# A new written order for the first two chunks of a fused attention and feed-forward kernel, with nine normalizing multiplications on GpSimd

## The chip, the cores and the metric

The kernel runs on one core of one Trainium2 chip. A core has five engines that matter here: TensorE (PE, matrix products), VectorE (DVE), ScalarE (ACT), GpSimd (POOL) and SyncE (SP), whose queue issues all loads and stores of this kernel. Every engine works through its own queue strictly in order; an instruction that waits holds up everything queued behind it on that engine, and nothing on the others. The metric is the device time of one execution in microseconds (us), lower is better.

## The reference

The reference computes attention for 4 batches, 8 heads, 768 rows and head size 64, and then a feed-forward layer on the 3072 rows of 512 that come out.

```python
k_sum = k.reshape(B, H, nb, 32, D).max(axis=3)          # 24 block maxima of the keys
v_sum = v.reshape(B, H, nb, 32, D).mean(axis=3)         # 24 block means of the values
scores_l = scale * q @ k.T, masked to |i - j| < 16      # window
scores_s = scale * q @ k_sum.T + log(32)
a = exp(concat(scores_l, scores_s) - rowmax)
a = a / (sum(a) + 1e-9)
x = a @ concat(v, v_sum)
h = x @ w_in;  r = max(h, 0);  g = s * r * r + b;  out = g @ w_out    # 512 -> 2048 -> 512
```

Inputs and output are float32. The products of the feed-forward layer are made to nearly full precision: each factor is split into an upper part and a remainder (in the tile type fp32r), and three products are summed, upper by upper, upper by remainder and remainder by upper.

## The kernel before

**Tiling.** The 3072 rows are cut into 12 chunks of 256 (three to a batch). A chunk passes through two stages. The attention stage goes by four pairs of heads `p`: for each, scores on PE, mask and row minimum on DVE, `exp` with row sums on ACT, normalization, a turn of the weights (by PE transposes in the first three chunks), and the products with the values on PE. A window of 96 keys and the 24 block maxima make rows of 120 weights; a pair's normalized tile `pr` is 128 x 4 x 120, that is 128 x 480. The feed-forward stage goes by 16 slices `f` of the inner dimension (128 wide): 12 products of 256 columns for the hidden rows, then for each two slices relu, square, scale and split, then 6 products of 512 columns for each slice into the output sums.

**Weights.** The weights come as raw 64-bit integers in the memory's layout, slice by slice (512 KB for each of the two sides). For each slice ACT rescales the two halves of the words (lines 122, 123), DVE joins them to a float (131, 132), DVE or ACT makes the upper part `wh` (219, 221 in a shared copy helper) and DVE the remainder `wl` (144). The hidden product of slice `f` cannot start before `wl` of that slice is there. This happens once, while the first two chunks run; later chunks find the weights in SBUF.

**What sets the order.** There is no scheduler: instructions are issued in the order in which the Python code calls the functions, and so each engine's queue is a piece of that order. For chunk 2's feed-forward stage and all later chunks the order comes from a table of steps. For chunks 0 and 1, together with the attention of chunk 2 and the first scores of chunk 3, it is written out by hand as a string of 450 names, `FIRST_ORDER`. A letter names the function, numbers its arguments (chunk, pair or slice), and asterisks choose another engine for the operation:

- `q` loads keys and queries of chunk 0, `u` those of later chunks, `x`, `v` the value windows, `r` whole value rows, `i`, `o`, `w` the weights of a slice (in, out, both), `s` copies the two scalars on POOL.
- `K` block maxima (DVE), `k` their copies into a pair's key tile (POOL), `Z`, `S` scores (PE), `M` mask (DVE, L323), `E` exps (ACT, L336), `N` normalize, `T` transposes (PE, L379), `C` copies the turned weights out (ACT, or DVE with an asterisk), `V`, `U` products with values and means (PE), `R`, `F` block means of the values (PE, then ACT or DVE), `t` their copies into a value window (POOL, L263), `X`, `y` upper part and remainder of the attention's result (`xh`, `xl`; L433 is `y` on DVE).
- `A`, `B`, `D`, `h`, `l` are the steps of the weights: rescale on ACT, join on DVE (halves and whole), upper part (ACT, or DVE with an asterisk), remainder on DVE.
- `Y`, `H` hidden products (PE; `Y` those of slices 0 and 1 of chunk 0 by pieces), `J` relu and square, `G` scale, `a`, `b` split, `P` output products (PE, L516), `O` copies the sums out and stores them, `W` a few products that only keep PE running.

`N` has three instructions: an addition of 1e-9 on 128 x 4 sums (L343), a reciprocal on DVE (L344) and the multiplication of the 128 x 480 tile (L346). In the kernel before an asterisk puts the addition on POOL, and the reciprocal and the multiplication are always on DVE.

**Places that the prediction speaks of.** `y1.3` is the last remainder of chunk 1's attention result, the eighth L433 row on DVE; it releases the hidden products of chunk 1 (`H1.0`, the first L460 row on PE). `V1.3` is chunk 1's last product with values; it waits for `t1.3`, a POOL copy. From `H1.0` on, PE has only large products in its queue with a little attention of chunks 2 and 3 between.

Of the kernel before, what the change touches and what calls it, by code (L numbers as in the profile page):

```python
# [19 lines left out]
P = 128  # L20
# [24 lines left out]
def windowed_attention_then_relu2_ffn(ctx, tc, qk, vwin, kt, vt, kq, vrow, wp, out):  # L45
# [107 lines left out]
    def k_max(bi, p):  # L153
        ksum[bi, p] = p2.tile([P, NB], F32, name="ksum", bufs=12)
        raw = kraw[bi, p]
        nc.vector.tensor_reduce(
            ksum[bi, p], raw.rearrange("p (n t) -> p n t", t=BLOCK), axis=AX.X, op=ALU.max
        )
# [181 lines left out]
    def normalize(c, p, other=False):  # L340
        mn_of.pop((c, p))
        rs = p2.tile([P, 4], F32, name="rs")
        (nc.gpsimd if other else nc.vector).tensor_scalar(rs, sm_of.pop((c, p)), 1e-9, None, ALU.add)  # L343
        nc.vector.reciprocal(rs, rs)  # L344
        pr = pr_of[c, p]
        nc.vector.tensor_tensor(pr, pr, rs.unsqueeze(2).to_broadcast([P, 4, KR]), ALU.mult)  # L346
# [186 lines left out]
    def evict(c, t, other=False):  # L533
# [184 lines left out]
```

## Time and profile before

| | us |
|---|---|
| median of 3 runs | 610.28 (610.14 to 610.51) |
| profiled execution | 611.14 |
| its span, from the first to the last instruction | 609.40 |
| PE busy in the span | 598.2 (98%) |
| DVE busy | 418.6 (69%) |
| ACT busy | 275.7 (45%) |
| POOL busy | 139.6 (23%) |

The granted TensorE clock is 1.00 in every stretch. A row of the timeline has the start, the duration, engine, source line, operation, the tile written and the tile read, the shape, how many instructions the row merges, and in square brackets how long the engine had been idle and what released it. A row of the groups has busy time and mean duration in ns behind the bar, then the idle time in front. A start of a following instruction can lie up to 0.1 us before the end of the one in front, since ends overlap.

### The profile page before, as it was taken

What the parts mean: (1) busy time and instruction counts of PE and PEld (TensorE: products, weight loads), DVE (VectorE), ACT (ScalarE), POOL (GpSimd) and SP (SyncE); (2) the same over time, 40 slices, a digit from 0 to 9 for tenths busy, and PEclk for the clock granted to TensorE, in tenths of its full rate; (3) what the DMA queues carried; (4) which work ended last, traced back from release to release, by engine and by line L of the source; (5) the groups of instructions that cost most, each with busy time, mean ns of one, the idle gap of its engine ahead of it and who ended that gap; (6) DMA issues with size and microseconds to landing.
All of it is one profiled execution on the core that took longest, in us unless ns stands there. A gap on an engine that the chain in (4) does not pass through costs nothing.

```text
span 609.4 us, 13484 instructions
## 1 busy us (share of the span) xinstructions
PE 598.2 (98%) x5240; PEld 539.5 (89%) x5240; DVE 418.6 (69%) x1126; ACT 275.7 (45%) x712; POOL 139.6 (23%) x275
## 2 busy tenths in 40 slices
PE   7999999999999999999999999999999999999997
PEld 6798988989888998999889899998998998898896
DVE  6999898789579368758858657847858827832211
ACT  5999898262362263163144244325235236223221
POOL 4420012211421411411041321231141151141110
PEclk9999999999999999999999999999999999999999
DMA  8998723026305015203502211600710500200000
GB/s 340 395 401 358 277 77 113 1 71 166 127 3 185 1 45 198 85 20 104 170 21 80 107 45 40 243 18 2 227 67 2 187 2 19 87 1 1 36 2 35
DMA packets 26993, 66.41 MB, mean 109 GB/s; under 512 B 3824, under 2 KB 3824, under 8 KB 26928
## 3 DMA queue, kind: packets, MB, share of 16 engines
q1 hardware_dynamic: 26928, 65.54, 30.3%
q8 instruction: 41, 0.67, 0.4%
q14 instruction: 24, 0.20, 0.1%
HBM read 59.09 MB, written 6.29 MB: 107 GB/s over the span
## 4 chain that ended last, share of the span: by engine, by line
PE 84%; ACT 7%; DVE 4%; issue 2%; DMA 2%; POOL 1%; SPq 0%; POOLq 0%; DVEq 0%; ACTq 0%
PE po L516 40%; PE ph L460 37%; PE pav L417 4%; PE ps L301 3%; ACT wraw L122 1%; ACT pr L336 1%; ACT wraw L123 1%; DVE wl L144 1%; DMA vsum<-vmean 1%; DVE wf L132 1%; POOL vw L263 1%; DMA kq<-in_kq_dram 1%; ACT r L468 1%; DVE wf L131 0%; PE pt L379 0%
## 5 line engine op out<-in xcount | busy, mean ns | idle before, releaser
L481 POOL TENSOR_SCALAR r<-r,sb_col 128x512 f32<-128x512 f32 x85 | 69.9, 823 | 386.5 <-ACT r L474 249.6
L468 ACT ACTIVATE r<-ph 128x512 f32<-128x512 f32 x93 | 55.5, 597 | 199.4 <-PE ph L460 144.0
L516 PE MATMUL po<-wh,gl 128*128 128x512 f32 x384 | 132.2, 394 | 0.0
L368 DVE STREAM_TRANSPOSE pT<-pr 32x256 f32<-32x256 f32 x288 | 125.4, 436 | 4.2
L460 PE MATMUL ph<-xh,wl 128*128 128x256 f32 x760 | 118.8, 279 | 0.5 <-ACT r L468 0.3
L460 PE MATMUL ph<-xl,wh 128*128 128x256 f32 x760 | 117.6, 277 | 0.0
L460 PE MATMUL ph<-xh,wh 128*128 128x256 f32 x760 | 117.4, 277 | 0.0
L460 PEld LDWEIGHTS ph<-xh,wl 128*128 128x128 f32 x760 | 104.7, 188 | 5.8 <-ACT r L474 0.7
L460 PEld LDWEIGHTS ph<-xl,wh 128*128 128x128 f32 x760 | 101.1, 188 | 0.0
L460 PEld LDWEIGHTS ph<-xh,wh 128*128 128x128 f32 x760 | 100.6, 188 | 0.0
L516 PEld LDWEIGHTS po<-wh,gl 128*128 128x128 f32 x384 | 72.1, 188 | 14.9 <-issue 1.1
L219 DVE CAST gha<-r 128x512 fp32r<-128x512 f32 x45 | 19.6, 437 | 89.1 <-POOL r L481 88.9
L336 ACT ACTIVATE pr<-pr,mn 128x120 f32<-128x120 f32 x176 | 67.0, 382 | 22.8 <-DVE mn L323 22.7
L516 PE MATMUL po<-wh,gha 128*128 128x512 f32 x192 | 75.3, 392 | 0.0
L516 PE MATMUL po<-wl,gha 128*128 128x512 f32 x192 | 75.3, 392 | 0.0
L516 PE MATMUL po<-wl,ghb 128*128 128x512 f32 x192 | 75.0, 391 | 0.0
L516 PE MATMUL po<-wh,ghb 128*128 128x512 f32 x192 | 75.0, 390 | 0.0
L474 ACT ACTIVATE r<-r 128x512 f32<-128x512 f32 x92 | 58.2, 633 | 5.7 <-DVE r L470 2.9
L263 POOL COPY vw<-vsum 24x256 f32<-24x256 f32 x88 | 47.3, 571 | 34.9 <-DMA vsum<-vmean 21.5
L219 DVE CAST ghb<-r 128x512 fp32r<-128x512 f32 x43 | 18.3, 426 | 43.9 <-POOL r L481 43.0
L516 PEld LDWEIGHTS po<-wh,gha 128*128 128x128 f32 x192 | 36.1, 188 | 7.8
L516 PEld LDWEIGHTS po<-wh,ghb 128*128 128x128 f32 x192 | 36.0, 188 | 7.8
(95 smaller groups left out, 667.7 us busy)
## 6 DMA issues: line engine op xcount, KB each, us to landing
wraw<-in_wp_dram SPq DMA_DIRECT2D x32, 512.0 KB
qk<-in_qk_dram SPq DMA_DIRECT2D x44, 369.0 KB
vw<-in_vwin_dram SPq DMA_DIRECT2D x48, 256.0 KB
out_dram<-o SPq DMA_DIRECT2D x24, 256.0 KB
kraw<-in_kt_dram SPq DMA_DIRECT2D x12, 384.0 KB
vraw<-in_vt_dram SPq DMA_DIRECT2D x12, 252.0 KB
kq<-in_kq_dram SPq DMA_DIRECT2D x4, 512.0 KB
vraw<-in_vt_dram SPq DMA_DIRECT2D x6, 264.0 KB
```

What stands on the lines that cost most here:

```text
L122: nc.scalar.activation(top, top, AF.Prelu, scale=2.0**-112, alpha=2.0**32)
L219: nc.vector.tensor_copy(out_, in_)
L263: nc.gpsimd.tensor_copy(vw_t[c, p][WIN:KR, e], vsum[bi][WIN : WIN + NB, 2 * p + e, :].unsqueeze(1).to_broadcast([NB, NSUB, D]),)
L301: nc.tensor.matmul(o, qi, kw[r, i, :], start=True, stop=True)
L336: nc.scalar.activation(pr, pr, AF.Exp, bias=mn_of[c, p][:, n : n + 1], scale=-1.0, accum_out=sm_of[c, p][:, n : n + 1])
L368: nc.vector.transpose(to[BLOCK * k : BLOCK * (k + 1), :, rows], src)
L417: nc.tensor.matmul(oi, vw[:KR, e, i, :], pi[:KR], start=True, stop=True)
L460: nc.tensor.matmul(ph, w[:, kc * P : (kc + 1) * P], x[:, kc], start=(n == 0), stop=(n == len(terms) - 1))
L468: nc.scalar.activation(r, ph, AF.Relu)
L474: nc.scalar.activation(r, r, AF.Square)
L481: (nc.vector if other else nc.gpsimd).tensor_scalar(g, g, s_col, b_col, ALU.mult, ALU.add)
L516: nc.tensor.matmul(po[c, t], g, w, start=t not in begun, stop=ends.get(t) == n)
```

## The change

`normalize` takes a second value of `other`: one asterisk puts the addition on POOL as before, two put the multiplication on POOL and leave the addition on DVE. `k_max` gets a switch to POOL that no name of the new order uses. All else is in `FIRST_ORDER`: the same 450 names in another order, with other asterisks on 54 of them.

```diff
-        (nc.gpsimd if other else nc.vector).tensor_scalar(rs, sm_of.pop((c, p)), 1e-9, None, ALU.add)
+        (nc.gpsimd if other == 1 else nc.vector).tensor_scalar(rs, sm_of.pop((c, p)), 1e-9, None, ALU.add)
         nc.vector.reciprocal(rs, rs)
         pr = pr_of[c, p]
-        nc.vector.tensor_tensor(pr, pr, rs.unsqueeze(2).to_broadcast([P, 4, KR]), ALU.mult)
+        (nc.gpsimd if other == 2 else nc.vector).tensor_tensor(pr, pr, rs.unsqueeze(2).to_broadcast([P, 4, KR]), ALU.mult)
...
-        "q1 S0.1.0 S0.1.1 K0.1 Z1 q0 S0.0.0 S0.0.1 q2 W1 K0.0 Z0 M0.1.0 q3 M0.1.1 M0.0.0 M0.0.1 E0.1.0 i0 K0.2 "
...
+        "q1 S0.1.0 S0.1.1 K0.1 Z1 M0.1.0 q0 K0.0 i0 M0.1.1 q2 q3 S0.0.0 S0.0.1 W1 Z0 M0.0.0 M0.0.1 E0.1.0 Ai0 W8 K0.2 "
...
```

Beside the normalizations the asterisks move these: the four copies of block means (`F`) from ACT to DVE; four upper parts `X` from ACT to DVE and one the other way; `h` five from ACT to DVE and two the other way; the relu or square of five `J` from DVE to ACT; six scalings `G` to ACT, two from ACT to POOL and two from ACT to DVE; two `C` and four `a` each way; and `O0.1` from DVE to ACT.

Three places show the move. On POOL, the first work behind the constants, with `rs` the reciprocals and `pr_...` the tiles of chunk 0. Before, then after:

```order
L343 TENSOR_SCALAR rs<-pr_201 128x4
L258 COPY qk<-ksum 128x4x24 x2
L343 TENSOR_SCALAR rs<-pr_288 128x4
L343 TENSOR_SCALAR rs<-pr_321 128x4
L258 COPY qk<-ksum 128x4x24
L193 COPY sb_col<-qk 128x2
```

```order
L193 COPY sb_col<-qk 128x2
L258 COPY qk<-ksum 128x4x24
L346 TENSOR_TENSOR pr_203<-pr_203,rs 128x480
L258 COPY qk<-ksum 128x4x24
L346 TENSOR_TENSOR pr_170<-pr_170,rs 128x480
L346 TENSOR_TENSOR pr_240<-pr_240,rs 128x480
L258 COPY qk<-ksum 128x4x24
L346 TENSOR_TENSOR pr<-pr,rs 128x480
L346 TENSOR_TENSOR pr_358<-pr_358,rs 128x480
L258 COPY qk<-ksum 128x4x24
L346 TENSOR_TENSOR pr<-pr,rs 128x480 x2
L263 COPY vw<-vsum 24x256 x2
```

The additions are gone from POOL, seven multiplications of chunks 0 and 1 stand between its copies, and the copy of the scalars, which needs the first `qk` load, has come to the head. On DVE, the first normalizations, before and after:

```order
L156 TENSOR_REDUCE ksum<-kq 128x24
L344 RECIPROCAL rs<-rs 128x4
L346 TENSOR_TENSOR pr_195<-pr_195,rs 128x480
L156 TENSOR_REDUCE ksum<-kq 128x24
L344 RECIPROCAL rs<-rs 128x4
L346 TENSOR_TENSOR pr_201<-pr_201,rs 128x480
```

```order
L343 TENSOR_SCALAR rs<-pr_170 128x4
L344 RECIPROCAL rs<-rs 128x4
L156 TENSOR_REDUCE ksum<-kq 128x24
L343 TENSOR_SCALAR rs<-pr_240 128x4
L344 RECIPROCAL rs<-rs 128x4
L323 ISA pr,mn<-ps,mask_mid 128x120
```

DVE now adds and inverts, and goes on to the next block without multiplying. On SP, the first loads (`kq` keys and queries of chunk 0, `wraw` weights, `qk` chunk 1's queries and keys, `vn` value rows, `vw` value windows), before and after:

```order
L240 DMA kq<-in_kq_dram 128x1024 x4
L114 DMA wraw<-in_wp_dram 128x1024 x2
L245 DMA qk<-in_qk_dram 128x738 x2
L187 DMA vn<-in_vrow_dram 128x1024 x3
L252 DMA vw<-in_vwin_dram 128x512
```

```order
L240 DMA kq<-in_kq_dram 128x1024 x2
L114 DMA wraw<-in_wp_dram 128x1024
L240 DMA kq<-in_kq_dram 128x1024 x2
L245 DMA qk<-in_qk_dram 128x738
L114 DMA wraw<-in_wp_dram 128x1024
L245 DMA qk<-in_qk_dram 128x738
L187 DMA vn<-in_vrow_dram 128x1024
L245 DMA qk<-in_qk_dram 128x738
L252 DMA vw<-in_vwin_dram 128x512
```

The first weights come ahead of the second half of chunk 0's keys, and the `qk` loads are spread among the others.

More of the change, by code (lines that the diff above doesn't have):

```diff
@@ L151, in load_k, with k_max @@
         nc.sync.dma_start(kraw[bi, p], kt[bi, p])
-    def k_max(bi, p):
+    def k_max(bi, p, other=False):
         ksum[bi, p] = p2.tile([P, NB], F32, name="ksum", bufs=12)
         raw = kraw[bi, p]
-        nc.vector.tensor_reduce(
+        (nc.gpsimd if other else nc.vector).tensor_reduce(
             ksum[bi, p], raw.rearrange("p (n t) -> p n t", t=BLOCK), axis=AX.X, op=ALU.max
```

43 rows, old and new, of the table FIRST_ORDER are left out of this document.

## The prediction

> **What bounds the kernel now.** I read the windows first, cut where PE's work changes, then the chain of waits, then the timeline of each engine in the first 37 us.
>
> ```profile
> core 0: us, PE busy (x) PEld busy (x) DVE busy (x) ACT busy (x) POOL busy (x), PEclk, DMA share, GB/s
> 0.00:4.26 4.26, 0.00 (x0) 0.00 (x0) 0.02 (x1) 1.28 (x1) 2.98 (x17) 1.00 0.56 202
> 4.26:36.64 32.38, 30.77 (x545) 25.07 (x545) 29.64 (x110) 27.53 (x94) 13.34 (x36) 1.00 1.01 393
> 36.64:125.66 89.02, 88.56 (x707) 79.27 (x706) 77.71 (x147) 71.75 (x132) 12.98 (x23) 1.00 0.50 191
> 125.66:605.86 480.20, 478.84 (x3993) 435.12 (x3991) 311.21 (x872) 174.53 (x487) 110.33 (x200) 1.00 0.22 73
> 605.86:609.40 3.54, 0.00 (x0) 0.00 (x0) 0.00 (x0) 0.59 (x1) 0.00 (x0) 1.00 0.38 148
> ```
>
> The stretches are: the wait for the first load; the attention of chunks 0 and 1 (up to `H1.0`); the feed-forward work of these chunks, with the weights being made; all the rest; and the last copy and store. In the fourth PE stands only 480.20 - 478.84 = 1.36 us, and nothing that the change touches runs there. The time can move in the second and third stretch.
>
> ```profile
> 36.64 0.62 PE L460 MATMUL ph<-xh,wl 128*128 128x256 f32 x4
> 223.46 5.47 PE ph L460 x48
> 228.92 5.47 PE po L516 x24
> ```
>
> The first row is `H1.0`, the others are two links of the chain in the steady part: a hidden product costs 5.47/48 = 0.114 us and an output product 5.47/24 = 0.228 us. PE's busy time hides waits, so I count its work. The third stretch holds 30 slices of hidden products (30 x 12 x 0.114 = 41.0; slices 0 and 1 of chunk 0 came before), 28 of output products (168 x 0.228 = 38.3) and some 7.4 of attention of chunks 2 and 3: 86.7 of 89.02 us. So **2.3 us** are lost there. The second stretch is another matter: PE runs 545 small products in 32.38 us, while DVE is busy for 29.64 (92%), ACT for 27.53 (85%), and the DMA engines all the time (share 1.01). It is DVE's queue that releases `H1.0`:
>
> ```profile
> 18.49 0.66 DVE L346 TENSOR_TENSOR pr<-pr,rs 128x480 f32<-128x480 f32 x1
> 34.31 0.69 DVE L131 TENSOR_SCALAR wf<-wraw 128x1024 uint32<-128x1024 uint32 x1
> 35.13 1.23 DVE L132 CUSTOM_DVE_ANT_0 wf<-wraw,wf 128x2048 uint16<-128x2048 uint16 x1
> 36.27 0.42 DVE L433 TENSOR_TENSOR xl<-pav,xh 128x256 fp32r<-128x256 f32 x1
> ```
>
> The last row is `y1.3`. None of these rows has idle time in front.
>
> **The change, part by part.** *DVE up to `y1.3`.* The order of rows up to the eighth L433 row gives the counts; durations come from the groups:
>
> ```profile
> L346 DVE TENSOR_TENSOR pr<-pr,rs 128x480 f32<-128x480 f32 x8 | 5.4, 672 | 1.0 <-ACT pr L336 0.5
> L219 DVE CAST wh<-wf 128x1024 fp32r<-128x1024 f32 x2 | 1.4, 686 | 0.0
> L219 DVE CAST xh<-pav 128x256 fp32r<-128x256 f32 x3 | 1.3, 418 | 0.0
> L323 DVE CUSTOM_DVE_ANT_0 pr<-ps,mask_mid 128x120 f32<-128x120 f32 x24 | 5.4, 277 | 0.0
> L343 DVE TENSOR_SCALAR rs<-sums 128x4 f32<-128x4 f32 x3 | 0.5, 169 | 3.6 <-ACT pr L336 3.6
> L221 ACT COPY vsum<-pm 24x128 f32<-24x128 f32 x4 | 1.0, 256 | 0.1
> ```
>
> Multiplications go from 8 to 1 (7 x 0.672 = -4.70), the upper part of slice 0's weights goes to ACT (-0.69), eight additions come from POOL (+8 x 0.169 = +1.35), four copies of means from ACT (+4 x 0.256 = +1.02, ACT's price for want of DVE's), one `xh` (+0.42) and two masks that now stand ahead (+0.55). Sum: **-2.2 us** of 29.64.
>
> *The seven multiplications on POOL.* The trace has none there. Its nearest rows have one tensor input:
>
> ```profile
> 141.11 0.77 POOL L481 TENSOR_SCALAR r<-r,sb_col 128x512 f32<-128x512 f32 x1 [7.45 <-ACT r L474]
> 143.94 1.28 POOL L481 TENSOR_SCALAR r<-r,sb_col 128x512 f32<-128x512 f32 x1 [2.06 <-issue]
> L263 POOL COPY vw<-vsum 24x256 f32<-24x256 f32 x16 | 10.3, 671 | 12.5 <-issue 7.8 <-DMA vw<-in_vwin_dram 4.5
> L258 POOL COPY qk<-ksum 128x96 f32<-128x96 f32 x12 | 4.3, 359 | 24.2 <-DMA qk<-in_qk_dram 16.8 <-DVE ksum L156 7.3
> ```
>
> Below: the rate of one input, 0.77 x 480/512 = 0.72 us. Above: two inputs as two passes, 1.44 us, stretched as the second row is against the first (1.28/0.77): 2.4 us. I take 1.2, between the two clear values and nearer the second. [...] Does POOL have room? Its written work from the first `qk` load to `t1.3` is the scalars' copy (0.7), four key copies (4 x 0.359 = 1.4), the seven multiplications, the two copies of `t1.0` (1.3), and then, behind chunk 2's first `qk` loads, two key copies (0.7) and six copies (4.0): 8.1 + 7x.
>
> ```profile
> 12.21 0.51 POOL L258 COPY qk<-ksum 128x96 f32<-128x96 f32 x1 [1.58 <-DMA qk<-in_qk_dram]
> 27.23 0.27 POOL L258 COPY qk<-ksum 128x96 f32<-128x96 f32 x1 [0.47 <-DMA qk<-in_qk_dram]
> 32.43 1.79 POOL L263 COPY vw<-vsum 24x256 f32<-24x256 f32 x2 [1.33 <-DMA vw<-in_vwin_dram]
> 34.88 0.69 PE L417 MATMUL pav<-pT,vw 120*64 120x64 f32 x16
> ```
>
> The first `qk` load now has one 512 KB load of weights less ahead of it, 0.52 MB / 0.393 MB per us = 1.3 us earlier than 12.21: 10.9. With x = 1.2 the work up to `t1.0` ends at 10.9 + 3.4 + 8.4 = 22.7, ahead of chunk 2's loads at about 27 to 28, and `t1.3` ends some 4.7 us behind those, at 32.6, where it now ends at 34.2. So POOL has cover of about 4 us; if that is gone (x above 1.8), each further 0.1 us costs 0.7.
>
> *Waits that the multiplications bring.* The turn `T` now waits for POOL instead of DVE, longer by 1.2 - 0.67 = 0.5 us for each pair; but pairs follow each other, and PE has small work between. Worse is the contention with DVE, which chunk 3's normalization shows beside a scaling on POOL:
>
> ```profile
> 131.36 0.16 DVE L343 TENSOR_SCALAR rs<-sums 128x4 f32<-128x4 f32 x1
> 131.64 2.02 POOL L481 TENSOR_SCALAR r<-r,sb_col 128x512 f32<-128x512 f32 x2 [15.60 <-DVE rs L343]
> 132.35 0.59 DVE L343 TENSOR_SCALAR rs<-sums 128x4 f32<-128x4 f32 x1
> 133.18 0.98 DVE L346 TENSOR_TENSOR pr<-pr,rs 128x480 f32<-128x480 f32 x1
> ```
>
> The addition takes 0.59 instead of 0.16 while POOL runs. If all eight additions were hit it would be 8 x 0.43 = 3.4 us, if none 0; most fall between multiplications, as each has to come first for its own, so I take two, +0.9. [...]
>
> *Loads.* The last value window of chunk 1 moves ahead of the weights of slice 2 (two of 512 KB), so `t1.3` finds its data 2.7 us earlier than at 32.43; slice 2's weights come 0.26 MB = 0.7 us later, at about the time when ACT takes them now, and slice 3's 0.75 MB = 1.9 us later. The join of slice 2 (now at 34.31) still stands ahead of `y1.3` on DVE, so that `y1.3` can't come much more than 1.2 us earlier: 2.2 - 0.9 = **1.3 us** earlier is what I take for `H1.0`, about 35.3. Bounds: 2.2 and, with all additions hit, -1.2.
>
> *The third stretch.* Of the 2.3 us lost two gaps are visible:
>
> ```profile
> 77.24 0.74 PE L460 MATMUL ph<-xh,wl 128*128 128x256 f32 x4 [0.29 <-ACT r L468]
> 83.21 0.71 PE L460 MATMUL ph<-xh,wl 128*128 128x256 f32 x4 [0.17 <-DVE wl L144]
> 81.93 1.15 DVE wl L144
> 74.03 1.12 ACT wraw L122
> ```
>
> The chain up to the second gap goes through DVE and ACT (the last two rows are links of it), so these two engines deliver just in time. Ahead of the seventh L144 row the new order has, beside the terms above, one scaling, one relu, one square and two `gh` less on DVE: about 1.9 us less again. That loosens the stretch, and the later raw weights tighten it (slice 4, whose weights are made at 44.91 to 47 now, gets its last side about 1.1 MB = 2.9 us later). I take **0.7** of 2.3 as regained; bounds 2.3 and a loss of 1.
>
> *Behind.* In chunk 3 PE waits once for POOL's copies of means:
>
> ```profile
> 165.72 0.33 PE L417 MATMUL pav<-pT,vw 120*64 120x64 f32 x2 [0.81 <-POOL vw L263]
> 166.53 1.61 PE L417 MATMUL pav<-pT,vw 120*64 120x64 f32 x46 [0.48 <-POOL vw L263]
> 122.45 0.69 DVE L219 COPY o<-po 128x512 f32<-128x512 f32 x1
> 124.17 0.40 ACT L336 ACTIVATE pr<-pr,mn 128x120 f32<-128x120 f32 x1 [1.80 <-DVE mn L323]
> ```
>
> The means depend on DVE's queue from chunk 3's masks on, which wait behind the copy of the third row; that copy is on ACT now, where 1.80 us were free. Up to 0.69 of these 1.29 us can go; I take **0.3**. The multiplications of chunk 2 (two on POOL) and the moved scalings lie where POOL is busy for 12.98 of 89.02 us: nothing.
>
> Sum: 1.3 + 0.7 + 0.3 = 2.3 us. 609.40 - 2.3 = 607.1 of span; the profiled execution lies 1.74 above its span and 0.86 above the median (611.14 against 610.28), so 607.1 + 1.74 - 0.86 = **608.0**.
>
> **The rivals.** *R1, DVE gives it back.* The additions and the joins wait behind POOL often (five or more of eight at 0.43 = 2.2 us), or the later weights hold ACT: `H1.0` comes when it does now and nothing is regained. For it: the rows at 131 to 133, and a DMA share of 1.01. Against: masks and maxima, most of DVE's work there, show no such stretch. Time: 609.9 (0.3 from behind).
>
> *R2, POOL becomes the bound, and the kernel is slower.* It decides from x = 1.8 on, where the work up to `t1.0` runs past chunk 2's loads, and breaks even with `t1.3` of today (34.2) at 10.9 + 8.1 + 7x = 34.2, x = 2.2. At the upper bound of 2.4 `t1.3` ends 1.6 us later than now, and `V1.3`, `X1.3` and `H1.0` with it; the third stretch regains nothing: 610.3 + 1.6 = 611.9. For it: 0.77 becomes 1.28 in this trace, and POOL stands at the foot of chains already. Against: before 36.64 POOL's neighbours on DVE are mostly short.
>
> *R3, more is regained.* With 1.9 us of room on DVE the third stretch loses only 0.5 of its 2.3 us, and the wait at 165 us goes by 0.7: 1.3 + 1.8 + 0.7 = 3.8, that is 606.5. For it: the gaps are all DVE's or ACT's. Against: some of the 2.3 us are small losses at each change between kinds of products, which stay.
>
> **How the numbers follow.** Forecast (607.0 to 609.0) 0.45, R3 0.17, R1 0.20, R2 0.18. A change is told from none from about 0.2% on, 1.2 us: faster is below 609.06, slower above 611.5. Faster: 0.45 + 0.17 = 0.62; R1 and a quarter of R2 are the same: 0.24; slower: 0.14. The range takes in R3 with 1.2 us to spare and R1, and most of R2: 605.3 to 611.5.
>
> **What would show it.** Right: the first L460 row at 35.0 to 35.8, POOL's L346 rows at 1.0 to 1.4 us, no wait of PE for POOL in the first 37 us over 0.5 us, first hidden product of chunk 2 at 123 to 124 instead of 125.66. R1: L343 rows of 0.5 us and more on DVE before 23 us, `y1.3` at 36 or later. R2: L346 rows of 1.8 us and more, and `V1.3` waiting for L263. The forecast is wrong if the third stretch grows: then the later weights, or ACT with its additional scalings, hold PE.

## The result, and the profile after

The changed kernel takes **614.65 us** (median of 6, 614.19 to 615.12) where the kernel before takes 610.26 (median of 6, 610.14 to 611.50): a ratio of 1.0072, 95% interval 1.0061 to 1.0083. It is slower by 4.4 us. The forecast was 608.0, range 605.3 to 611.5.

The windows of the changed kernel, cut at the same pieces of work as those of before (front; the first products of `H1.0`; feed-forward of chunks 0 and 1; the rest; the end). The columns are those of the windows in the prediction.

```profile
4.26:37.57 33.31, 29.48 (x544) 24.73 (x545) 27.18 (x115) 25.14 (x87) 16.37 (x35) 1.00 0.92 342
37.57:40.53 2.96, 1.48 (x11) 1.08 (x10) 2.54 (x4) 2.83 (x6) 1.40 (x2) 1.00 1.02 411
40.53:129.43 88.90, 88.70 (x698) 80.33 (x697) 76.08 (x140) 71.93 (x131) 11.02 (x21) 0.98 0.52 194
129.43:609.80 480.37, 479.22 (x3992) 435.40 (x3992) 311.26 (x874) 174.80 (x488) 110.04 (x200) 1.00 0.22 73
609.80:613.30 3.50, 0.00 (x0) 0.00 (x0) 0.00 (x0) 0.50 (x1) 0.00 (x0) 1.00 0.39 150
```

The third row ends at the same product as the row 36.64 to 125.66 of before. The products from 40.53 on are those that ran from 37.55 on before: `H1.0` is **2.98 us late**. The third stretch takes 88.90 us where the same work took 125.66 - 37.55 = 88.11 (+0.8); the fourth 480.37 against 480.20. So 2.98 of the 3.9 us by which the span grew (613.3 against 609.4) are made in the first 40 us. There PE stood for 33.31 - 29.48 + 2.96 - 1.48 = 5.3 us; before, for 32.38 - 30.77 = 1.6 us. The same stretch, now cut on both sides at the end of `y1.3`, before and then in the change:

```profile
4.24:36.69 32.45, 30.82 (x545) 25.12 (x546) 29.71 (x110) 27.58 (x94) 13.36 (x36) 1.00 1.01 393
```

```profile
4.24:40.25 36.01, 30.73 (x551) 25.58 (x551) 29.46 (x119) 27.69 (x92) 17.79 (x37) 1.00 0.93 347
```

PE, VectorE and ScalarE have nearly the work that they had; VectorE's is smaller by 0.25 us only. The stretch is 3.56 us longer, and all of that is waiting.

The rows of the change that show PE's first stops, in the timeline of the engines (the bracket is the idle time in front and what ended it):

```profile
16.52 0.99 POOL L346 TENSOR_TENSOR pr<-pr,rs 128x480 f32<-128x480 f32 x1 [0.38 <-DVE rs L344]
16.68 0.86 DVE L343 TENSOR_SCALAR rs<-sums 128x4 f32<-128x4 f32 x1
18.25 0.28 DVE L323 CUSTOM_DVE_ANT_0 pr<-ps,mask_mid 128x120 f32<-128x120 f32 x1
18.59 0.75 PE L301 MATMUL ps<-qk 64*64 64x120 f32 x16 [1.59 <-DVE mn L323]
24.73 0.63 PE L301 MATMUL ps<-qk 64*64 64x120 f32 x8 [0.65 <-DVE mn L323]
25.29 0.65 PE L379 MATMUL pt<-ident,pr 128*120 128x128 f32 x4
```

The scores of chunk 1's third unit (18.59) need two PSUM tiles, and the pool of score tiles has two. They come free with the last mask of the second unit, `M1.1.1`, the row at 18.25. The new order writes that mask behind the first unit's normalization, whose addition took 0.86 us beside a multiplication on POOL, and behind a pair of masks of chunk 0. At 24.73 PE waits for a mask again: `S1.3.1`, in the order of before right behind `S1.3.0`, is now written behind `M1.3.0` and waits for it. Behind it in PE's queue stands the turn `T1.0` (25.29).

And the rows that show the end of the front (SPq rows are issues of loads; L252 loads value windows, L114 weights):

```profile
26.60 2.84 SPq L252 DMA_DIRECT2D vw<-in_vwin_dram  x3
29.49 0.90 SPq L114 DMA_DIRECT2D wraw<-in_wp_dram  x2
35.89 0.67 ACT L122 ACTIVATE wraw<-wraw 128x512 f32<-128x512 f32 x1 [1.58 <-DMA wraw<-in_wp_dram]
37.85 0.69 DVE L131 TENSOR_SCALAR wf<-wraw 128x1024 uint32<-128x1024 uint32 x1 [1.66 <-ACT wraw L122]
38.69 1.23 DVE L132 CUSTOM_DVE_ANT_0 wf<-wraw,wf 128x2048 uint16<-128x2048 uint16 x1
39.83 0.42 DVE L433 TENSOR_TENSOR xl<-pav,xh 128x256 fp32r<-128x256 f32 x1
40.30 0.39 PE L460 MATMUL ph<-xl,wh 128*128 128x256 f32 x1 [0.87 <-DVE xl L433]
```

The same load before the change, and two lines of the waits of SP's queue over the whole span, of before and then of the change (total, times, longest):

```profile
24.19 0.90 SPq L114 DMA_DIRECT2D wraw<-in_wp_dram  x2
```

```profile
SPq L252 <- PE pav L415: 2.9, 2, 1.6
```

```profile
SPq L252 <- PE pav L415: 6.3, 2, 3.7
```

The three value windows `x1.1` to `x1.3` wait on SP's queue for buffers, which PE's value products of chunk 0 free (L415). Slice 2's weights are queued behind them and are issued 5.3 us later than before. ScalarE then waits 1.58 us for them, VectorE waits 1.66 us for ScalarE with the join of these weights, and `y1.3` stands behind that join: 39.83 instead of 36.27.

This is one execution. The profile of a second one (612.28 to 616.31 us in that batch, the profiled one 615.57) has its ninth product just as late, at 40.47, and gets there otherwise: the wait of 1.59 us is one of 0.19, the join waits for nothing, and PE's work up to there is 34.32 us of 36.27, largely because its products between 13.75 and 20 us took about 1.6 times as long as in the first (rows of this kind are shown at the end).

### The profile page after: what moved, and what is told of

Read it like the earlier page. It is cut to its first block, busy times and chain, and to the rows that moved or that the text cites. A ratio compares the mean times of both kernels' runs of the same rounds, so it can differ in the third digit from the quotient of the medians.

```text
span 613.3 us, 13508 instructions
## 1 busy us (share of the span) xinstructions
PE 598.9 (98%) x5240; PEld 541.5 (88%) x5240; DVE 417.1 (68%) x1129; ACT 276.5 (45%) x710; POOL 141.8 (23%) x274
## 4 chain that ended last, share of the span: by engine, by line
PE 85%; DVE 5%; DMA 3%; ACT 2%; issue 1%; SPq 1%; POOL 1%; POOLq 0%; ACTq 0%; DVEq 0%
PE po L516 39%; PE ph L460 38%; PE pav L417 3%; PE ps L301 3%; DMA vsum<-vmean 2%; DVE pT L368 2%; ACT pr L336 1%; DMA wraw<-in_wp_dram 1%; POOL vw L263 1%; SPq L180 1%; PE warm L199 1%; DMA kq<-in_kq_dram 1%; DVE pr L323 1%; DVE gl L497 0%; DVE ksum L156 0%
## 5 line engine op out<-in xcount | busy, mean ns | idle before, releaser
L460 PE MATMUL ph<-xh,wl 128*128 128x256 f32 x760 | 119.1, 279 | 0.8 <-ACT xh L221 0.6
L460 PE MATMUL ph<-xl,wh 128*128 128x256 f32 x760 | 118.5, 278 | 0.9 <-DVE xl L433 0.9
L460 PE MATMUL ph<-xh,wh 128*128 128x256 f32 x760 | 118.0, 278 | 0.0
L460 PEld LDWEIGHTS ph<-xh,wl 128*128 128x128 f32 x760 | 105.1, 188 | 6.0 <-ACT xh L221 0.8
L460 PEld LDWEIGHTS ph<-xl,wh 128*128 128x128 f32 x760 | 101.8, 189 | 1.1 <-DVE xl L433 1.1
L460 PEld LDWEIGHTS ph<-xh,wh 128*128 128x128 f32 x760 | 101.2, 189 | 0.0
L474 ACT ACTIVATE r<-r 128x512 f32<-128x512 f32 x95 | 60.1, 633 | 3.6 <-DVE r L470 0.6
L263 POOL COPY vw<-vsum 24x256 f32<-24x256 f32 x88 | 45.8, 554 | 25.1 <-DMA vsum<-vmean 22.1
```

The source lines that it names most:

```text
L263: nc.gpsimd.tensor_copy(vw_t[c, p][WIN:KR, e], vsum[bi][WIN : WIN + NB, 2 * p + e, :].unsqueeze(1).to_broadcast([NB, NSUB, D]),)
L460: nc.tensor.matmul(ph, w[:, kc * P : (kc + 1) * P], x[:, kc], start=(n == 0), stop=(n == len(terms) - 1))
L474: nc.scalar.activation(r, r, AF.Square)
```

## The experiments

Three theories. **A**: the load order; slice 2's weights stand behind windows that wait for buffers, and their join delays `y1.3`. **B**: the multiplications on POOL hold the chain. **C**: PE is the bound of the front, and each wait of PE for a score tile counts in full (and holds the windows' buffers too). A fourth came in later, **K**: stretches in which the granted clock of PE reads 0.50. In the diffs "..." leaves out steps between, and names with stars are steps on another engine (`N` with two stars: the multiplication on POOL; with one: the addition on POOL). "Ninth product" is the row that answers to 37.55 before and 40.53 in the change, the ninth product of `H1.0`. Behind each median stand the lowest and the highest run, behind each ratio its 95% interval; the ratio is to the kernel before in the same batch of runs.

### The change with one piece undone

**Slice 2's weights ahead of all three windows.**

```diff
-... E1.3.1 x1.1 y1.0 ... y1.1 l1 V1.2 w2 X1.2* ...
+... E1.3.1 w2 x1.1 y1.0 ... y1.1 l1 V1.2 X1.2* ...
```

> The new order with one name moved: the load of slice 2's weights (w2) stands ahead of the last three value windows of chunk 1 (x1.1 to x1.3) instead of behind them. Theory A (SP's queue is held by value windows that wait for a free buffer, and the weights behind them come 5 us late): slice 2's weights are issued at about 23 to 25 us instead of 29.5, ACT no longer waits for them, y1.3 comes at 36.5 to 37.5 instead of 39.83, and the time falls by 2 to 3 us, to about 612. Theory B (the multiplications on GpSimd hold the chain): the time stays within 0.7 us of 614.65. Theory C (PE's queue is held by the second halves of scores that now wait for masks): the same as B.

615.46 (612.51 to 619.36), ratio to before 1.0067 (1.0042 to 1.0092). Rows of its timeline:

```profile
24.88 0.90 SPq L114 DMA_DIRECT2D wraw<-in_wp_dram  x2
28.73 1.73 SPq L252 DMA_DIRECT2D vw<-in_vwin_dram  x3
35.66 1.02 PE L417 MATMUL pav<-pT,vw 120*64 120x64 f32 x16 [1.49 <-POOL vw L263]
```

The weights come when they came before, ScalarE no longer waits for them, and now the value products wait for windows; `y1.3` comes at 41.70. Nothing is gained. This execution also ran at half clock from 19.3 to 22.8 us (0.51 in that window), so its times in the front do not say how much of the lateness the load made.

**The multiplications back on VectorE.** All `N` steps with the engines of before, in the new order.

```diff
-... N0.0** ... N0.1** ... N1.2** ... N1.3 ...
+... N0.0* ... N0.1* ... N1.2* ... N1.3* ...
```

> The new order with the normalizations on the engines of the kernel before: all multiplications on DVE, the additions on GpSimd. Theory A: DVE has 4 us more work ahead of y1.3 but waits 1.7 us and 0.8 us there for ACT, so 614.6 to 616.5. Theory B: 611 to 612. Theory C: the same as A.

617.56 (615.07 to 620.97), ratio 1.0106 (1.0074 to 1.0138). PE's wait for `M1.1.1` is 1.90 us there instead of 1.59. B, which expected 611 to 612, falls. That the multiplications on POOL help within the new order is likely, not shown: the interval overlaps those of the change (1.0061 to 1.0083, and 1.0041 to 1.0078 in its second measurement).

**Scaling and join of slice 2 behind `X1.3` and `y1.3`.**

```diff
-... w3 A2* t1.3 V1.3 X1.3 D2 Y1.3 k2.2 J0.0 w5 y1.3 H1.0 ...
+... w3 t1.3 V1.3 X1.3 A2* Y1.3 k2.2 J0.0 w5 y1.3 D2 H1.0 ...
```

> The new order with slice 2's rescaling (A2, ACT) behind X1.3 and its join (D2, DVE) behind y1.3, so that the attention of chunk 1 no longer stands behind late weights on these two engines. Theory A in its plain form (slice 2 late): the two waits of PE in H1.0 (1.5 us) go, but PE waits for slice 2 four products later instead, 613.5 to 614.5. If the place of the join in the two queues is what turns the late load into a wait: 612 to 613. Theories B and C: y1.3 no earlier than 38, 614 to 615.

616.79 (615.67 to 619.82), ratio 1.0088 (1.0056 to 1.0120). `y1.3` does come earlier, at 38.35, and the ninth product at 39.20 instead of 40.53; then PE stands for 2.74 us ahead of 43.91, and a half-clock window follows (mean granted clock of the execution 0.997; an output product at 48.03 takes 0.63 us, one at 49.26 takes 0.39). In this execution the gain ahead of `H1.0` is lost behind it; no theory had expected more than 615 us.

**Second halves of scores right behind their first halves** (`S0.2.1`, `S1.2.1`, `S1.3.1`).

```diff
-... S0.2.0 Z2 M0.2.0 S0.2.1 ... S1.2.0 r2 S1.2.1 ... S1.3.0 N1.2** X0.0* i1 M1.3.0 S1.3.1 ...
+... S0.2.0 S0.2.1 Z2 M0.2.0 ... S1.2.0 S1.2.1 r2 ... S1.3.0 S1.3.1 N1.2** X0.0* i1 M1.3.0 ...
```

> The new order with the second half of a pair's scores put back right behind the first (S0.2.1, S1.2.1, S1.3.1), so that no mask stands between the halves. Theory C: PE's waits for masks at 12.2 and 24.7 us go (0.4 and 0.65 us), T1.0 comes at 24.3 instead of 25.3, and with it everything behind, the value windows too: 612.5 to 613.5. Theory A: the same, since the buffers of the value windows come free by PE's queue, but the gain stays under 1.5 us. Theory B: 614 to 615.

613.07 (611.14 to 618.16), ratio 1.0041 (1.0014 to 1.0067). The wait at 24.7 is gone, the one of 1.59 us stays.

### Order and engines apart

**The order of before, only the nine multiplications on POOL.**

```diff
-... N0.1* ... N0.0* ... N0.2* ... N2.1 ...
+... N0.1** ... N0.0** ... N0.2** ... N2.1** ...
```

> The order of before in every step; only the nine multiplications are on GpSimd, as in the change. If the multiplications are what costs (theory B), this alone is slower than before by 2 us or more: 612 to 614. If the written order costs (theories A and C), the multiplications are worth what they take off DVE: seven times 0.67 us less the additions that they stretch (1.4 us): 607 to 610.5.

611.01 (610.36 to 612.31), ratio 1.0015 (1.0003 to 1.0028): if anything slower, by 0.15% or 0.9 us. This run bears most directly on the prediction's main term: seven multiplications leave VectorE ahead of `y1.3`, and eight additions come to it, as in the change. Its timeline, and its window from the first product to `H1.0`:

```profile
32.55 0.42 DVE L433 TENSOR_TENSOR xl<-pav,xh 128x256 fp32r<-128x256 f32 x1 [1.10 <-ACT xh L221]
36.78 0.42 DVE L433 TENSOR_TENSOR xl<-pav,xh 128x256 fp32r<-128x256 f32 x1
37.14 0.62 PE L460 MATMUL ph<-xh,wl 128*128 128x256 f32 x4
```

```profile
4.17:37.14 32.97, 30.86 (x545) 24.93 (x545) 28.97 (x111) 27.24 (x94) 16.92 (x35) 1.00 1.01 376
```

`y1.3` starts at 36.78, against 36.27 before, and `H1.0` at 37.14 against 36.64. The relief of VectorE is small: 28.97 us of work against 29.64, for the additions came back, and rows beside POOL's work are longer (a join of weights at 11.75 takes 1.26 us where it took 0.69, one at 23.00 takes 1.12 where it took 0.50). VectorE now has pauses (1.10 us ahead of 32.55, for ScalarE's copy, which waits for PE), and PE waits for POOL three times (0.33, 0.36 and 0.44 us). PE's work is as full as before: 30.86 of 32.97 us. So the multiplications on POOL do not bring the term; what a clean relief of VectorE would bring, this run does not show.

**The new order with every step on its old engine** (54 steps).

```diff
-... N0.0** ... C0.1* ... F1 F0 F2 ... X0.0* ... h6* ... G0.2* ...
+... N0.0* ... C0.1 ... F1* F0* F2* ... X0.0 ... h6 ... G0.2** ...
```

> The order of the change in every step; every step on the engine that it had before. If the written order costs (A and C), it stays slow without any engine move: 615 to 618, as with the multiplications back on DVE alone (617.6). If the engine moves cost (B), it comes back to 609 to 612.

631.22 (627.23 to 633.93), ratio 1.0349 (1.0319 to 1.0379), far above what any theory expected. Three lines of its waits of PE up to 140 us (total, times, longest):

```profile
PE ps L301 <- DVE mn L323: 3.7, 3, 1.9
PE ph L460 <- DVE wl L144: 3.5, 5, 2.1
PE po L516 <- DVE gl L497: 2.3, 3, 1.4
```

**The old order with every step on its new engine**, the same steps the other way round.

> The order of before in every step, every step on the engine that the change gives it (multiplications, additions, copies, squares, scalings). If the engines that the change picks are a gain by themselves and only the order costs: 608 to 611. If the picks suit only their own order: slower than before by 2 us or more, 612 to 620, as the new order on the old engines was (631.2).

616.32 (615.96 to 617.54), ratio 1.0097 (1.0072 to 1.0121). Here POOL is waited for:

```profile
25.74 0.65 PE L379 MATMUL pt<-ident,pr 128*120 128x128 f32 x4 [1.25 <-POOL pr L346]
32.84 1.02 PE L417 MATMUL pav<-pT,vw 120*64 120x64 f32 x16 [0.54 <-POOL vw L263]
```

The order alone costs 21 us, the engines alone 6, both together 4.4. So the effects of the parts do not add up, and terms worked out for one part at a time can't be summed.

**The loads alone.** The change with the front's loads in the order that they had before, and the kernel before with the loads in the new order (first keys and queries, rows, windows, slices 0 to 3). The loads alone, of before with - and of the change with +:

```diff
-q1 q0 q2 q3 i0 o0 u1.0 u1.1 r0 r1 r2 v0 u1.2 i1 v1 v2 u1.3 x1.0 o1 v3 u2.0 u2.1 x1.1 x1.2 w2 x1.3 w3
+q1 q0 i0 q2 q3 u1.0 o0 u1.1 r0 u1.2 v0 r1 r2 u1.3 v3 i1 v2 x1.0 v1 o1 u2.1 u2.0 x1.1 x1.2 x1.3 w2 w3
```

> The change, with the loads of the front (first keys and queries, rows, windows of chunks 0 and 1, weights of slices 0 to 3) in the order that they had before; work of the other engines as in the change. Theory A in its wide form (the order of loads on SP's queue makes means, windows and weights late): most of the loss goes, 609 to 612. Theory C (the order of small products on PE and of masks holds PE, and the buffers come free late from that): 613.5 to 616.

> The order and engines of before; only the loads of the front stand in the order of the change. Theory A in its wide form: the loss is here, 612.5 to 615. Theory C: 609 to 611.5, since PE frees the buffers as early as before.

615.21 (612.55 to 617.66), ratio 1.0083 (1.0057 to 1.0109), and 614.81 (612.67 to 616.60), ratio 1.0078 (1.0057 to 1.0099). A's wide form is half right: the new order of loads alone makes the kernel before slower by about 5 us. In its trace a value product of chunk 0 waits for its window:

```profile
24.65 1.12 PE L415 MATMUL pav<-pT,vw 96*64 96x64 f32 x16 [1.58 <-DMA vw<-in_vwin_dram]
```

But giving the change its old loads back does not mend its median. Again loads and order can't be judged apart. (Two of these six executions, with a mean granted clock of 1.00, took 612.55 and 612.56 us; the other four, at 0.994 to 0.997, took 614.68 to 617.66. Six runs are too few to tell a gain that half-clock windows hide from none.)

### Mending PE's waits

**`M1.1.1` right behind `M1.1.0`**, ahead of the first unit's normalization.

```diff
-... M1.1.0 Ao0 N1.0** S0.3.0 S0.3.1 Z3 M0.3.0 E0.3.0 M1.1.1 E1.1.1 ...
+... M1.1.0 M1.1.1 Ao0 N1.0** S0.3.0 S0.3.1 Z3 M0.3.0 E0.3.0 E1.1.1 ...
```

> The change with one step moved: the second pair of masks of chunk 1's second unit right behind its first pair on VectorE, ahead of the normalization of the first unit and of the masks of chunk 0's last. The two PSUM tiles of its scores are what the third unit's scores wait for (1.59 us). Theory C (PE's small products are the bound of the front, each wait of PE counts in full): about 1.4 us less than the change, 612.5 to 613.7. Theory A (only the late weights of slice 2 and their joins set the end): 614 to 615, as the change.

614.07 (611.74 to 615.52), ratio 1.0060 (1.0043 to 1.0077). The wait goes from 1.59 to 0.77 us and the ninth product from 40.53 to 39.52. The median lies where A expected it, not C: against the change's ratios, 1.0072 and 1.0060, no gain can be told.

**And the three second halves adjacent**, the edit shown above.

> As the run with the mask early, and the second halves of three scores right behind their first halves. Theory C: both waits of PE gone (1.59 and 0.65 us): 611 to 612.7. Theory A: 613.5 to 615.

612.75 (611.20 to 613.75), ratio 1.0039 (1.0024 to 1.0054). From its timeline:

```profile
18.44 0.74 PE L301 MATMUL ps<-qk 64*64 64x120 f32 x16 [0.77 <-DVE rs L344]
36.41 0.70 DVE L131 TENSOR_SCALAR wf<-wraw 128x1024 uint32<-128x1024 uint32 x1 [0.29 <-ACT wraw L122]
37.49 0.62 PE L460 MATMUL ph<-xh,wl 128*128 128x256 f32 x4
```

The ninth product is at 39.08. No load was moved, and yet the join waits 0.29 us instead of 1.66. In the median this is as much as the halves alone gave (1.0041), so the early mask shows in the traces only.

**And slice 2's weights ahead of the last window.**

```diff
-... x1.3 y0.1 Y0.1 Y0.2 X1.1 y1.1 l1 V1.2 w2 X1.2* ...
+... w2 x1.3 y0.1 Y0.1 Y0.2 X1.1 y1.1 l1 V1.2 X1.2* ...
```

> As the run before it, and slice 2's weights loaded ahead of chunk 1's last value window, as before the change. If what is left over the kernel before is the late weights (theory A for the rest): 1 to 2 us less than without, 609.5 to 611.5. If the window then comes late in their place: no difference.

612.52 (611.06 to 615.85), ratio 1.0038 (1.0022 to 1.0054). From its timeline:

```profile
26.24 0.90 SPq L114 DMA_DIRECT2D wraw<-in_wp_dram  x2
33.26 0.70 ACT L122 ACTIVATE wraw<-wraw 128x512 f32<-128x512 f32 x1
36.67 0.63 PE L460 MATMUL ph<-xh,wl 128*128 128x256 f32 x4
37.85 0.63 PE L460 MATMUL ph<-xh,wh 128*128 128x256 f32 x4
```

ScalarE has no wait for the weights any more, and the ninth product is at 37.85: of the 2.98 us that `H1.0` was late, 0.30 are left. The span of this execution is 609.3, as before the change (609.4), but it is the fastest of the twelve (611.06 us). The median did not follow: it lies where it lay without the moved load.

**The weights ahead of the last window alone**, the last edit without the two mends on PE.

> The change with one load moved: slice 2's weights ahead of chunk 1's last value window only (before the change they stood there too), nothing else. Theory A alone: the wait of 1.58 us of ScalarE for these weights goes and with it most of the joins' delay: 612 to 613. Theory C (PE's waits in front hold the products that free the windows' buffers): 613.5 to 615, the load gains where masks come early, and little here.

614.36 (611.67 to 617.66), ratio 1.0046 (1.0019 to 1.0073), not told apart from the change. The weights are issued at 30.71, for the windows ahead of them still wait for buffers; the ninth product is at 40.79. While PE's waits stand, A shows no gain of its own (this execution, too, had a half-clock window in the front, 0.50 from 19.4 to 22.7 us).

### What is left: half-clock windows?

**Unused products in PE's idle places**, in the mended kernel and in the change (`W1` ahead of `S1.0.0`; `W1`, or `W3` in the change, ahead of `S1.2.0`), and the kernel before without its four single ones.

```diff
-... M0.2.1 r0 E0.0.1 E0.0.0 S1.0.0 S1.0.1 ... r1 Bo0 S1.2.0 ...
+... M0.2.1 r0 E0.0.1 E0.0.0 W1 S1.0.0 S1.0.1 ... r1 Bo0 W1 S1.2.0 ...
```

> As the run with masks early, halves adjacent and slice 2's weights ahead of the last window, and one unused product of the identity on PE in each of two idle places of 0.59 and 0.77 us (ahead of the scores of chunk 1's first and third unit). If half-clock windows behind PE's idle places are what still costs (theory K), the times gather at the low end: 610.5 to 611.5. If not, 612 to 613 as without.

> The change, with unused products of the identity in its idle places on PE: one ahead of the scores of chunk 1's first unit, three (1.3 us) in the 1.59 us ahead of the third's. Theory K: the times gather at the low end, 612.5 to 613.7. Theory C alone: 614 to 615.2, since the waits stay.

> The kernel before without its four single unused products on PE (the eight in one piece stay): PE has less to do. Theory K: half-clock windows come in at some executions, the spread grows and the median rises by 0.5 to 2 us: 610.5 to 612. Without theory K: same or less, 608.5 to 610.2.

> The change itself once more, beside the others of this batch: 613.8 to 615.2.

Mended and filled: 611.82 (610.72 to 613.26), ratio 1.0029 (1.0018 to 1.0039). The change filled: 614.84 (612.16 to 616.33), ratio 1.0063 (1.0043 to 1.0084). The change again: 613.92 (612.28 to 616.31), ratio 1.0060 (1.0041 to 1.0078). The kernel before without them: 610.04 (608.74 to 612.09), ratio 0.9995 (0.9983 to 1.0007). Filling does not help the change, opening does not hurt the kernel before: half-clock windows are not shown to be what is left. The mean granted clock that every run lists says more. One window of 3.4 us at half clock takes 0.3% off it (the first profiled execution of the change has such a window and a mean of 0.997). All twelve executions of the mended and filled kernel, all twelve of the mended one without the moved load and all six of the change's second measurement have 0.999 or 1.000. So windows that this clock shows are not what is left; such as it misses are not excluded. The last kernel shows something else:

```profile
35.74 0.62 PE L460 MATMUL ph<-xh,wl 128*128 128x256 f32 x4
```

Four products less on PE, and `H1.0` starts 0.9 us earlier than before (36.64) in this execution, though VectorE is busy as before: 29.56 of the 31.49 us up to there, PE only 28.35. Before, PE was the fuller of the two. This fits PE as the bound of the front, with VectorE close behind. The third stretch gave some of it back (chunk 2's first product at 125.11 instead of 125.66), and the median has nothing of it.

**The front of before, then the change.** Order and engines of before up to `H1.0`, then the steps that are left as in the change.

> Order and engines of before up to the first whole hidden product of chunk 1, and from there the steps that are left in the order and on the engines of the change. If the change's loss is all in the front, and its later part a small gain (0.7 in the third stretch and 0.3 at 165 us in the prediction): 608.5 to 610.2. If the later part loses as well: 611 to 614.

624.54 (623.00 to 629.20), ratio 1.0218 (1.0176 to 1.0260). The seam made a wait of its own, 11.05 us of PE for key windows of chunk 2 (the row is shown at the end), so this does not tell what the later part of the change is worth.

The runs side by side (ratio to the kernel before in the same batch; "ninth product" in the profiled execution, where PE's first product starts between 4.05 and 4.28 us, so that 0.2 us between two rows say nothing):

| kernel | ratio | ninth product, us |
|---|---|---|
| before | 1 | 37.55 |
| the change | 1.0072, again 1.0060 | 40.53, again 40.47 |
| `M1.1.1` early | 1.0060 | 39.52 |
| and halves adjacent | 1.0039 | 39.08 |
| and weights of slice 2 ahead of the last window | 1.0038 | 37.85 |
| and two unused products | 1.0029 | 37.71 |
| weights ahead of the last window alone | 1.0046 | 40.79 |
| only the multiplications on POOL | 1.0015 | 38.04 |

None of them is faster than the kernel before.

## Why the prediction was wrong

**The step that failed is the first: "It is DVE's queue that releases `H1.0`", with "None of these rows has idle time in front".** The four rows have none, but none of them says who waits for `y1.3`. In the kernel before, nobody did:

```profile
37.09 0.62 PE L460 MATMUL ph<-xl,wh 128*128 128x256 f32 x4
37.55 0.62 PE L460 MATMUL ph<-xh,wh 128*128 128x256 f32 x4
```

`H1.0` multiplies the upper parts `xh` first. The remainders `xl` enter with its fifth product, and `y1.3`, the last of them, with the eighth: it does not release the first L460 row. `H1.0` started at 36.64, ahead of the end of `y1.3` at 36.69, and the rows above have no idle time in front either. PE came to `H1.0` through its own queue, busy for 30.77 of 32.38 us, more than VectorE's 29.64; the prediction passed over that as "another matter". While PE's work stays the same, its 1.6 us of waits are all that a relief of the other engines can gain. In the change PE does wait for `y1.3`, 0.87 us ahead of 40.30.

**The relief was mis-sized too.** The six terms that were summed to -2.2 us make -2.05, and with the contention of +0.9 the prediction took -1.3. VectorE's work up to the end of `y1.3` fell by 0.25 us. The stretched additions (below) took 1.4 us of the 2.05, the copies of means, at 1.22 instead of 1.02 us, another 0.2. What grew is the waiting: VectorE stood for 6.55 us of the stretch where it had stood for 2.74. The term was 1.3 us earlier for `H1.0`, and its ninth product came 2.98 later. The multiplications by themselves, in the order of before, make the kernel longer if anything, by some 0.9 us.

**"Waits that the multiplications bring": the wrong waits were priced.** The turns' waits for POOL are 0.39 us at most in the change, as expected. What was not looked at is what the new order does to PE's queue: where each mask stands on VectorE against the scores that need its PSUM tiles. Two tiles, and a mask that slid behind another unit's normalization, cost PE 1.59 us of waiting; a second half written behind a mask 0.65. Mending both brought the ninth product from 40.53 to 39.08 and 1.3 to 2 us of the median (ratio 1.0072 or 1.0060 to 1.0039), though the intervals of the second measurement and of the mended kernel overlap.

**"Slice 2's weights come 0.26 MB = 0.7 us later": sized by bytes, and the queue waited for buffers.** They were issued 5.3 us later (29.49 against 24.19). The windows that moved ahead of them need buffers that PE's products free, and PE was late. So this error seems to hang on the one above: with PE's waits mended the join waits 0.29 us without any load moved, and moving the load alone gained nothing that can be told. Together they took the ninth product back to 37.85, in one execution. In the second execution of the change the join (37.82) waits for nothing, and `y1.3` stands at 39.78 all the same: the weights are not the whole of it.

**The price on POOL was right, the cover was there.** The group rows of the change:

```profile
L346 POOL TENSOR_TENSOR pr<-pr,rs 128x480 f32<-128x480 f32 x9 | 8.9, 988 | 20.9 <-DVE rs L344 16.5 <-ACT pr L336 3.9 <-ACT r L474 0.4
```

0.99 us each, where 1.2 was taken (bounds 0.72 and 2.4). The copies of `t1.3` end at 33.5 (32.6 in the prediction). R2 did not come true in the change. With the new engines in the old order PE does wait for POOL, 2.0 us in the front, but the mark of R2, rows of 1.8 us, is not there either: the mean is 1.04.

**The contention was undersized.** Four additions were stretched, to 0.40, 0.86, 0.45 and 0.39 us from 0.16 to 0.17: 1.4 us in all, where 0.9 was taken. The row of 0.86 has `M1.1.1` behind it.

**The third stretch** was to regain 0.7 us. It lost 0.8 in the first profiled execution, which has a half-clock window of 3.4 us there (up to 1.7 us by itself, an estimate: half of 3.4), and regained 0.2 in the second (87.92 against 88.11). In the two mended kernels with the weights of slice 2 early it regained 0.6 (87.47 and 87.49), in the one without it nothing (88.27); with the multiplications alone on POOL, in the order of before, it regained 1.0 (87.11). The sign may be right where the weights come in time; no run settles it, for the one that should have failed at its seam.

**The wait at 165 us** was to shrink by 0.3 of 1.29:

```profile
169.13 0.33 PE L417 MATMUL pav<-pT,vw 120*64 120x64 f32 x2 [0.37 <-POOL vw L263]
169.94 1.61 PE L417 MATMUL pav<-pT,vw 120*64 120x64 f32 x46 [0.48 <-POOL vw L263]
```

0.85 are left, 0.44 less: right.

**The rivals.** R1 named the later weights on ScalarE as a cause and `y1.3` at 36 or later as its mark, and that is what the trace shows; it allowed for no loss, since the only loss in the list was POOL's. The chance of slower, 0.14, hung on POOL's price alone. A rival "PE's own queue waits" was missing, and it is the one that fits the first trace and the mends best; the second trace, with slower products and few waits, came to the same lateness. The small losses between kinds of products, which spoke against R3, are in the trace of before: the four hidden products at 61.45, behind scores, take 0.58 us up to the next four, those at 62.03 take 0.45.

**What stays open.** With the mends the profiled execution, the fastest of its twelve, is back at the span of before; the median is 1.6 to 2.5 us above it. What the other executions have more was not in any trace that tells it. Two things seen in single executions could be part of it, both below: products that are slow while the clock column reads 1.00, and late means. And the wait of 1.59 us, the largest, is shown to move the ninth product in one trace, not the median.

## What to carry to other kernels

That an engine has no idle time ahead of a row does not show that anybody waits for the row: one looks at the row that reads it, whether it starts at once and has idle time in front. Before an engine's relief is counted, one looks at the fullest queue of the stretch, PE's too where its products are small. Taking a little work off each engine in turn, and counting what each then really has to do, tells more than the sum of the rows that were moved. When an order changes, each buffer pool of two is a place to look at: which step frees the tile, and behind what does that step now stand on its engine. A load that moves behind others is late by their waits for buffers too, not only by their bytes (here 5.3 us, where 0.7 was taken by bytes).

## What the runs showed of the hardware

**A half-clock window behind gaps of PE.** Two windows of the change, next to each other (the third column from the end is the granted clock):

```profile
37.90:41.30 3.40, 1.92 (x14) 1.54 (x13) 3.26 (x9) 3.24 (x6) 1.40 (x2) 1.00 1.03 416
41.30:44.70 3.40, 3.40 (x36) 3.18 (x39) 3.26 (x12) 3.09 (x5) 0.00 (x0) 0.50 1.02 416
```

PE was busy for 1.92 of 3.4 us, and for the next 3.4 us it got half the clock: up to 1.7 us lost (an estimate: half of 3.4), twice the wait of 0.87 us ahead of it. In the run with the weights ahead of all windows it came after 1.85 busy us of 3.4, with the halves adjacent after 1.77, with the new loads in the old order after 1.84 (and for 6.8 us there). The kernel with an 11 us wait shows four such lengths (first the row of the wait, then the window):

```profile
50.63 2.20 PE L301 MATMUL ps<-qk 64*64 64x120 f32 x32 [11.05 <-POOL qk L258]
```

```profile
42.30:55.90 13.60, 5.27 (x45) 4.56 (x46) 10.90 (x12) 5.74 (x6) 3.74 (x4) 0.50 0.95 372
```

The lengths here are 3.4 us and multiples of it (6.8, 13.6). In the first four cases the stretch of 3.4 us ahead was not idle, PE was busy for about half of it. Less work did not always bring it: with the multiplications back on VectorE one stretch of 3.4 us had only 1.01 us of work and no half clock behind it (the scores at 20.18 took 0.75 us, as those at 18.59 in the change). What decides is not shown.

**The clock column may miss it.** In the change with the old loads, score products took 1.08 us for what takes 0.75 at 20.32, while the column reads 1.00:

```profile
14.43 1.08 PE L301 MATMUL ps<-qk 64*64 64x120 f32 x16
17.02 1.08 PE L301 MATMUL ps<-qk 64*64 64x120 f32 x16
20.32 0.75 PE L301 MATMUL ps<-qk 64*64 64x120 f32 x16 [0.18 <-DVE mn L323]
```

The second execution of the change shows the same from 13.75 to about 20. In the recorded half-clock window above, 32 score products took 1.64 us where 32 took 1.05 at 31.00, a like factor; that these rows ran at half clock is argued from this, not shown.

**The stretched additions end with the multiplication.** The addition at 16.68 ends at 17.54, the multiplication beside it at 16.52 + 0.99 = 17.51; the ones at 15.76 and 21.70 end 0.02 us behind theirs as well. So in these three cases an addition on VectorE lasted as long as what POOL had left. Others beside POOL did not: masks, whose scores come from PSUM, kept their 0.25 to 0.28 us, and a reduction of keys from SBUF at 14.93 its 0.92 beside the multiplication at 15.15. What holds the additions is not shown. The longest was stretched by 0.69 us (0.86 instead of 0.17), more than the 0.43 that the prediction took from one row, the other two by 0.23 and 0.28.

**The means of a later chunk can come 2 us late.** In the second execution of the change, a copy at 311 us waits for a small transfer of block means, where before the change it hardly waited (first row: before; second: the change again):

```profile
306.75 1.10 POOL L263 COPY vw<-vsum 24x256 f32<-24x256 f32 x3 [0.31 <-DMA vsum<-vmean]
```

```profile
311.18 1.09 POOL L263 COPY vw<-vsum 24x256 f32<-24x256 f32 x3 [2.07 <-DMA vsum<-vmean]
```

PE then waits 0.91 and 0.48 us for POOL. The first execution of the change has 0.2 us there and the mended kernel with unused products 1.35, so it changes from one execution to the next; one profile for each kernel can't tell how often.
